# Gated recurrence and FFT gate on one core: transposes of 128 rows in place of pairs of 64 rows, with s and u in a bank each

## The chip, the cores and the metric

The kernel runs on one core of one Trainium2 chip. The metric is the device time of one execution in microseconds (us). The core's engines are named as the profile names them: PE is TensorE's matmul, PEld its load of weights, DVE VectorE, ACT ScalarE, POOL GpSimd and SP SyncE, which issues the DMAs here.

## The reference

Two layers, one after the other. The first is a gated recurrence along the sequence (6272 steps, 256 channels, 4 batches). The second multiplies two projections of its result with a circular convolution of a third one, and projects once more.

```python
def _attn_ref(x, f_logit, lower_bound):
    sig = 1.0 / (1.0 + np.exp(-f_logit))
    f = lower_bound[None, None, :] + (1.0 - lower_bound[None, None, :]) * sig
    i = 1.0 - f
    for t in range(S):
        h = f[:, t] * h + i[:, t] * x[:, t]
        y[:, t] = h

def _moe_ref(x, w_proj, filter_fft, w_out):
    proj = x @ w_proj
    x1, x2, x3 = (proj[..., :D], proj[..., D:2 * D], proj[..., 2 * D:])
    X2 = np.fft.rfft(x2, n=S, axis=1)
    H = np.fft.rfft(filter_fft, n=S, axis=0)[None, :, :]
    x2_conv = np.fft.irfft(X2 * H, n=S, axis=1)
    y = x1 * x2_conv * x3
    return y @ w_out
```

## The kernel before

All work is written as a list of operations: `op(...)` records a function, the engines that may run it and what it reads and writes. A table, `ORDER`, names for every operation its place in the program, its engine and its first PSUM bank. `emit` walks the table and calls the functions in that order, so the order on each engine and the banks are fixed by hand; `ROWS` and `ANY` name kinds of operations for a choice in `emit` that no kind uses here, since `ANY` is empty. PSUM is one tile, `PS`, of 128 x 8 banks x 512 fp32 columns. An operation with `take=1` holds one bank, one with `take=2` two neighbouring banks, `pb` and `pb + 1`. The framework adds the semaphores for what the instructions read and write.

The recurrence is `hgrn(b)`, in 13 chunks of 512 steps (the last has 128). A chunk of f_logit and one of x are loaded with 128 partitions of four consecutive steps (`FL`, `XT`, three buffers each, L321). ACT makes s = sigmoid(-f_logit) in place (L324), POOL makes u = x * s in place (L326). For each half `kh` of the channels:

- su, on PE (L338): s and u are turned, so that channels are on partitions and steps along the row. Each 128 x 128 block is turned in two transposes of 64 rows (the loop over `p`), with a 64 x 64 part of the identity. The weights that PE loads are the data; the identity streams. The output goes to every `nb`-th column (four for a full chunk). The first half of s goes to the start of the first bank and the second half to columns 256 to 511 of the second; u lies between them, across the border of the two banks: `(0, 768)` and `(512 - hn, 512)` are the columns where the halves begin, and `hn` is 256. So the two halves of a block go to different banks.
- f, on ACT (L351) or DVE (L353): f = 1 - (1 - lower_bound) * s is read from the two runs of s (`halves`) and written to `fTs`.
- scan, on DVE (L359): the recurrence itself, with f from `fTs` and u from PSUM, written as fp16 to `HA`. It begins with the last column of the chunk before. The factor (1 - lower_bound) of i is put into the weights of the second layer.
- wrap (POOL, ACT or SP): a copy of the first part of `HA` behind its end.

The second layer of batch b runs beside this: P (L707) and F1 (L720), the first steps of the transform; mini (L736) and F2 (L779), on 64 rows each; the product with the filter's spectrum (L800 on DVE, L809 on POOL); I2 (L819) and I1 (L853, on 64 rows), the inverse; x13 (L387), the two projections that are multiplied in; the product y (L859 on DVE); proj (L871) and its copy and store. The filter's own spectrum is prepared once at the start (L624, L649, L667, L684), and L595 are matmuls that keep PE at work. `hgrn(b + 1)` stands behind batch b in the list of operations, and the table mixes its operations with those of batch b: in time, transposes run from 30 to 76 us, and in the stretches 120 to 181, 220 to 281 and 300 to 380 us.

The functions that the change touches:

Of the kernel before, what the change touches and what calls it, by code (L numbers as in the profile page):

```python
# [13 lines left out]
AOP = mybir.AluOpType  # L14
AF = mybir.ActivationFunctionType
# [43 lines left out]

class Plan:  # L60

    ROWS = ("su", "F2", "mini", "I1", "FF2", "last")
    ANY = ()
    ENGINES = ("ACT", "DVE", "PE", "POOL", "SP", "MUL")

# [9 lines left out]
    def op(self, kind, cost, fn, r=(), w=(), dma=0.0, lag=0.0, table=None, take=0, src=None, part=None, margin=0.0):  # L75
        preds = set()
        for t in r:
            if t in self.writer:
                preds.add(self.writer[t])
        for t in w:  # L80
            if t in self.writer:
                preds.add(self.writer[t])
            preds.update(self.readers.get(t, ()))
        me = len(self.ops)
        if src is not None:
            preds.add(src)
            self.ops[src]["users"].append(me)
        self.ops.append(dict(kind=kind, batch=self.batch, cost=cost, fn=fn, preds=preds, dma=dma, lag=lag,
                             table=table, take=take, src=src, part=part, margin=margin, users=[]))
        for t in r:  # L90
            self.readers.setdefault(t, set()).add(me)
        for t in w:
            self.writer[t] = me
            self.readers[t] = set()
        return me
# [10 lines left out]
    def emit(self):  # L106
        rows, seen = False, set()
        for i, e, b in self.order():
# [8 lines left out]
            elif e == "PE":  # L117
                rows = o["kind"] in self.ROWS
            o["fn"](*args)
# [74 lines left out]
def kernel(  # L194
# [10 lines left out]
    nc = tc.nc  # L205
# [4 lines left out]
    op = plan.op  # L210

    konst = ctx.enter_context(tc.tile_pool(name="konst", bufs=1))
    iden = konst.tile([128, 128], F32, name="iden")
    omc = konst.tile([128, 2], F32, name="omc")
    nomc = konst.tile([128, 2], F32, name="nomc")
# [32 lines left out]
    FF2 = [("FF2", u) for u in range(NU)] + ["FF2"]  # L248
# [5 lines left out]
    PS = psp.tile([128, 8, 512], F32, name="PS")  # L254
# [23 lines left out]
    def copy(e, dst, src, scale=None):  # L278
        if e == "ACT":
            if scale is None:  # L280
                nc.scalar.copy(dst, src)  # L281
            else:
                nc.scalar.activation(dst, src, AF.Copy, scale=scale)  # L283
        elif e == "DVE":
            if scale is None:
                nc.vector.tensor_copy(dst, src)
            else:
                nc.vector.tensor_scalar(dst, in0=src, scalar1=scale, scalar2=None,
                                        op0=AOP.mult)
        elif e == "SP":  # L290
            nc.sync.dma_start(dst, src)
        else:
            nc.gpsimd.tensor_copy(dst, src)
# [5 lines left out]
    def bank(pb):  # L299

        return PS[:, pb:pb + 2].rearrange("p a t -> p (a t)")

    def halves(pb, hn):

        a = PS[:, pb, 0:hn]
        return bass.AP(tensor=a.tensor, offset=a.offset,
                       ap=[a.ap[0], [768, 2], a.ap[1]])

    count = dict(x=0, f=0, s=0, o=0, u=0, h=0)


    def hgrn(b):
        for c in range(NCHK):
            t0 = c * CH
            nb = min(CH, S - t0) // 128
            n = nb * 128
            k = count["x"] % NX
            count["x"] += 1
            xt, ft = XT[:, k, 0:nb], FL[:, k, 0:nb]
            for dst, src, t in ((ft, f_logit, ("ft", k)), (xt, x, ("xt", k))):  # L320
                op("load", {"SP": 0.46}, lambda e, dst=dst, src=src, t0=t0, n=n: nc.sync.dma_start(  # L321
                    dst, src[b, t0:t0 + n, :].rearrange("(p j) d -> p j d", p=128)),
                   w=[t], dma=0.38 * nb, lag=2.4, margin=MARGIN)
            op("sig", {"ACT": 0.095 + 0.213 * nb}, lambda e, ft=ft: nc.scalar.activation(  # L324
                ft, ft, AF.Sigmoid, scale=-1.0), w=[("ft", k)], table="sigmoid")
            op("u", {"POOL": 0.1 + 0.553 * nb}, lambda e, xt=xt, ft=ft: nc.gpsimd.tensor_tensor(  # L326
                xt, xt, ft, op=AOP.mult), r=[("ft", k)], w=[("xt", k)])
            for kh in range(2):
                cols = slice(kh * 128, kh * 128 + 128)

                hn = 64 * nb

                def turn(e, pb, ft=ft, xt=xt, cols=cols, nb=nb, hn=hn):
                    for src, at in ((ft, (0, 768)), (xt, (512 - hn, 512))):
                        for j in range(nb):
                            for p in range(2):
                                ps = slice(64 * p, 64 * p + 64)
                                nc.tensor.transpose(bank(pb)[:, at[p] + j:at[p] + hn:nb],  # L338
                                                    src[ps, j, cols], iden[ps, ps])
                su = op("su", {"PE": 0.126 * nb}, turn, r=[("ft", k), ("xt", k), "iden"], w=["qT"], take=2)  # L340
                j = count["f"] % 2
                count["f"] += 1
                fT = fTs[:, j, 0:n]
                t1 = HB[kh] + t0
                h = HA[:, t1:t1 + n]

                def gate_f(e, pb, fT=fT, hn=hn, kh=kh):
                    by, sT = nomc[:, kh:kh + 1], halves(pb, hn)
                    fT = fT.rearrange("p (a t) -> p a t", a=2)
                    if e == "ACT":  # L350
                        nc.scalar.activation(fT, sT, AF.Identity, scale=by, bias=1.0)  # L351
                    else:
                        nc.vector.tensor_scalar(fT, in0=sT, scalar1=by, scalar2=1.0,  # L353
                                                op0=AOP.mult, op1=AOP.add)
                op("f", {"ACT": 0.145 + n / 1200.0, "DVE": 0.11 + n / 960.0}, gate_f,
                   r=["om"], w=[("fT", j)], src=su)
                init = 0.0 if c == 0 else HA[:, t1 - 1:t1]
                op("scan", {"DVE": 0.12 + 2.08 * n / 1000.0}, lambda e, pb, h=h, fT=fT, hn=hn, init=init:
                   nc.vector.tensor_tensor_scan(h, fT, bank(pb)[:, 512 - hn:512 + hn], init, op0=AOP.mult,  # L359
                                                op1=AOP.add),  # L360
                   r=[("fT", j)] + ([("hn", kh, c - 1)] if c else []), w=[("hn", kh, c)],
                   src=su)

                z = min(t0 + n, WR)
                if z <= t0:
                    continue
                op("wrap", {"POOL": 0.05 + (z - t0) / 1015.0, "ACT": 0.08 + (z - t0) / 1200.0, "SP": 0.46},
                   lambda e, a=t0, z=z, o=HB[kh]: copy(
                       e, HA[:, o + S + a:o + S + z], HA[:, o + a:o + z]),
                   dma=0.5, lag=2.0,  # L370
                   r=[("hn", kh, c)], w=[("W", kh, i) for i in range(t0 // 1024, (z - 1) // 1024 + 1)])
# [514 lines left out]
    with tc.manual_schedule():  # L886
        scope = ctx.enter_context(ExitStack())
        prepare(scope.enter_context(tc.tile_pool(name="tmp", bufs=1)))
        hgrn(0)

        def turn(e):

            scope.close()
            cv = ctx.enter_context(tc.tile_pool(name="cv", bufs=1))

            late["zt"] = cv.tile([128, 2, Q, 128], F16, name="zt")
            late["Th"] = cv.tile([128, TB, 2, 64], F16, name="Th")
            late["ys"] = cv.tile([128, 2, 2, 512], F32R, name="ys")
            late["x1s"] = cv.tile([128, 2, CH], F32, name="x1s")
            late["x3s"] = cv.tile([128, 2, CH], F32, name="x3s")  # L900
            late["osb"] = [cv.tile([128, 4, 256], F32, name=f"osb{i}") for i in range(NO)]
        op("pre", {"SP": 0.01}, turn, r=FF1 + FF2 + ["ID", "VA", "FT1", "D1", "VB"], w=["cv"])

        for b in range(B):
            plan.batch = b
            spectrum(b)
            gate(b)
            phase_o(b)
            if b + 1 < B:
                plan.batch = b + 1  # L910
                hgrn(b + 1)
        plan.emit()
# [30 lines left out]
```

## Time and profile before

| what | value |
|---|---|
| median of 3 runs | 470.0 us (467.44 to 473.95) |
| the profiled execution | 470.84 us |
| its span, first to last instruction | 469.1 us |
| mean granted TensorE clock | 0.993 |
| PE, busy share of the span | 95% |
| DVE | 89% |
| ACT | 86% |
| POOL | 67% |
| PE on the transposes of s (L338, FL) | 784 matmuls, mean 230 ns |
| PE on the transposes of u (L338, XT) | 784 matmuls, mean 223 ns |
| DVE on the scan (L359) | 96 of 113.0 us, mean 1202 ns, and 8 more (the first chunks) |
| ACT on f (L351) | 90 of 59.4 us, mean 680 ns |

The span is what the trace shows of one execution; the time of the execution has 1.7 us more around it. Busy time is the union of an engine's instructions. Matmuls overlap each other, so the mean duration of one is not what it costs: this is read from the distance between the starts of two that follow each other. "A <- B: 5.2, 13, 1.1" in the list of waits means that A sat idle until B ended, 5.2 us in 13 waits, of which the longest was 1.1 us.

### The profile page before, as it was taken

To read this page: it belongs to the slowest core of one execution; us is meant where nothing else is said; L and a number is where in the kernel's file an instruction comes from. 1 tells how busy PE (TensorE), PEld (TensorE's weight loads), DVE (VectorE), ACT (ScalarE), POOL (GpSimd) and SP (SyncE) were. 2 spreads that over 40 slices of the span, in tenths; PEclk is the share of its full clock that TensorE was granted. 3 is DMA by queue.
4 is the path that set the end of the run, shared out by engine and by line. 5 is a ranking of instruction groups with operands and counts; after the bars stand their busy time and mean duration, and the time that the engine had idled before them with its cause. 6 is when DMAs were issued, how large, how long until landed. Compare 5 with 4: busy or idle time off the path is not lost.

```text
span 469.1 us, 14729 instructions
## 1 busy us (share of the span) xinstructions
PE 444.2 (95%) x6041; PEld 348.9 (74%) x6041; DVE 417.2 (89%) x477; ACT 405.4 (86%) x581; POOL 313.0 (67%) x293
## 2 busy tenths in 40 slices
PE   8779889899989999999999989999999999999998
PEld 6667666767766789777767879667778898777787
DVE  8679988599989998699999998899999987999873
ACT  4989987789989998799999987999999876999664
POOL 5988865268989854485999441878998512887700
PEclk9799999999999999999999999999999999999999
DMA  8967888957597999256787989377697831554167
GB/s 334 395 244 265 309 296 245 306 195 211 197 250 243 337 308 346 108 187 211 240 271 276 304 310 337 106 226 224 190 315 274 306 153 46 169 164 156 65 264 286
DMA packets 40417, 113.40 MB, mean 242 GB/s; under 512 B 4322, under 2 KB 6754, under 8 KB 40350
## 3 DMA queue, kind: packets, MB, share of 16 engines
q1 hardware_dynamic: 40350, 112.47, 70.1%
q8 instruction: 47, 0.77, 0.6%
q14 instruction: 20, 0.16, 0.1%
HBM read 80.93 MB, written 31.00 MB: 239 GB/s over the span
## 4 chain that ended last, share of the span: by engine, by line
PE 65%; DVE 16%; ACT 8%; issue 6%; DMA 3%; POOL 1%; ACTq 0%; DVEq 0%; POOLq 0%
PE PS L387 14%; PE PS L707 8%; PE PS L819 8%; PE PS L871 7%; DVE HA L359 7%; PE PS L338 6%; PE PS L779 6%; PE PS L720 5%; DVE ys L859 4%; DMA FL<-in_f_logit_dram 3%; PE PS L595 3%; PE PS L853 3%; PE PS L624 2%; PE PS L649 2%; ACT HA L281 2%
## 5 line engine op out<-in xcount | busy, mean ns | idle before, releaser
L326 POOL TENSOR_TENSOR XT<-XT,FL 128x1024 f32<-128x1024 f32 (+1 forms) x52 | 117.1, 2253 | 60.3 <-ACT FL L324 50.8
L359 DVE TENSOR_TENSOR_SCAN HA<-fTs,HA,PS 128x512 f16<-128x512 f32 (+1 forms) x96 | 113.0, 1202 | 4.1 <-ACT fTs L351 3.4
L800 DVE TENSOR_TENSOR PP<-PS,Hu 98x1008 f16<-98x1008 f32 x89 | 103.6, 1199 | 1.9 <-DMA Hu<-H 0.7
L387 PE MATMUL PS<-HA,W 128*128 128x490 f16 (+1 forms) x416 | 100.2, 367 | 1.7 <-ACT HA L281 0.8
L417 POOL TENSOR_TENSOR zt<-x1s,x3s 128x490 f16<-128x490 f32 (+1 forms) x48 | 58.5, 1224 | 40.2 <-DVE ys L859 11.6
L809 POOL TENSOR_TENSOR PP<-HA,Hu 98x1008 f16<-98x1008 f16 x39 | 81.8, 2105 | 2.7 <-ACT HA L281 1.7
L281 ACT CAST HA<-PS 128x1024 f16<-128x1024 f32 (+1 forms) x90 | 75.4, 865 | 7.8 <-PE PS L720 4.8
L859 DVE TENSOR_TENSOR ys<-PS,zt 128x1024 fp32r<-128x1024 f32 (+1 forms) x52 | 58.7, 1154 | 4.6 <-PE PS L853 2.5
L351 ACT ACTIVATE fTs<-PS,nomc 128x512 f32<-128x512 f32 (+1 forms) x90 | 59.4, 680 | 2.8 <-PE PS L338 1.6
L283 ACT ACTIVATE osb<-PS 128x1024 f32<-128x1024 f32 (+1 forms) x52 | 50.4, 981 | 13.1 <-PE PS L871 6.6
L387 PEld LDWEIGHTS <-W 128*128 128x128 f16 x416 | 35.6, 97 | 33.9 <-issue 7.3
L324 ACT ACTIVATE FL<-FL 128x1024 f32<-128x1024 f32 (+1 forms) x52 | 53.0, 1020 | 8.9 <-DMA FL<-in_f_logit_dram 8.9
L871 PE MATMUL PS<-Wo,ys 128*128 128x256 f32 x392 | 56.8, 291 | 0.2 <-DVE ys L859 0.2
L819 PEld LDWEIGHTS <-PP 98*128 98x128 f16 x1024 | 49.3, 98 | 10.1 <-issue 3.1
L283 ACT ACTIVATE x1s<-PS 128x490 f32<-128x490 f32 (+1 forms) x87 | 50.6, 591 | 5.2 <-PE PS L387 3.8
L819 PE MATMUL PS<-VA,PP 98*128 98x98 f16 x512 | 51.9, 207 | 0.6 <-DVE HA L359 0.5
L871 PEld LDWEIGHTS PS<-Wo,ys 128*128 128x128 f32 x392 | 49.1, 188 | 4.0 <-DVE ys L859 0.6
L819 PE MATMUL PS<-VB,PP 98*128 98x98 f16 x512 | 51.6, 207 | 0.0
L281 ACT CAST Th<-PS 128x784 f16<-128x784 f32 x57 | 46.9, 829 | 3.1 <-PE PS L819 2.2
L338 PE MATMUL PS<-iden,FL 64*128 64x64 f32 x784 | 44.7, 230 | 3.9 <-DVE HA L359 1.5
L338 PEld LDWEIGHTS PS<-iden,FL 64*128 64x128 f32 x784 | 33.5, 138 | 16.9 <-DVE HA L359 5.2
L707 PE MATMUL PS<-W,HA 128*128 128x256 f16 x392 | 44.3, 273 | 1.8 <-ACT X L281 1.8
(114 smaller groups left out, 744.9 us busy)
## 6 DMA issues: line engine op xcount, KB each, us to landing
FL<-in_f_logit_dram SPq DMA_DIRECT2D x48, 512.0 KB
XT<-in_x_dram SPq DMA_DIRECT2D x48, 512.0 KB
out_dram<-osb SPq DMA_DIRECT2D x48, 512.0 KB
Hu<-H SPq DMA_DIRECT2D x55, 392.0 KB
X<-in_moe_filter_fft_dram SPq DMA_DIRECT2D x9, 512.0 KB
H<-Hu SPq DMA_DIRECT2D x8, 196.0 KB
Hu<-in_moe_filter_fft_dram SPq DMA_DIRECT2D x2, 512.0 KB
H<-Hu SPq DMA_DIRECT2D x8, 128.0 KB
```

The source lines that it names most:

```text
L281: nc.scalar.copy(dst, src)
L283: nc.scalar.activation(dst, src, AF.Copy, scale=scale)
L326: op("u", {"POOL": 0.1 + 0.553 * nb}, lambda e, xt=xt, ft=ft: nc.gpsimd.tensor_tensor(xt, xt, ft, op=AOP.mult), r=[("ft", k)], w=[("xt", k)])
L338: nc.tensor.transpose(bank(pb)[:, at[p] + j:at[p] + hn:nb], src[ps, j, cols], iden[ps, ps])
L359: nc.vector.tensor_tensor_scan(h, fT, bank(pb)[:, 512 - hn:512 + hn], init, op0=AOP.mult, op1=AOP.add),
L387: nc.tensor.matmul(PS[:, p, 0:n], W13[:, kh, js], HA[:, HB[kh] + t0:HB[kh] + t0 + n], start=(kh == 0), stop=(kh == 1))
L707: nc.tensor.matmul(pp[:, r - r0, :], column(HB[kh], q_of(r)), W2[:, kh, :], start=(kh == 0), stop=(kh == 1))
L800: nc.vector.tensor_tensor(pr, px.unsqueeze(1).broadcast_to([TB, 2, UE, 63]), hh, op=AOP.mult)
L809: nc.gpsimd.tensor_tensor(pr, spec[:, o, :, 1:64].unsqueeze(1).broadcast_to([TB, 2, UE, 63]), hh, op=AOP.mult)
L819: nc.tensor.matmul(PS[:, ib + o, pr * TB:(pr + 1) * TB], PP[:TB, k, o, n, 2 * pr:2 * pr + 2, :], v[:TB], start=(n == 0), stop=(n == 1))
L859: nc.vector.tensor_tensor(late["ys"][:, yk, :, 0:rn * 128], PS[:, cb:cb + 2, 0:rn * 128], late["zt"][:].rearrange("p k r m -> p k (r m)") ...
L871: nc.tensor.matmul(po[:, i, :], late["ys"][:, yk, kh, i * 128:(i + 1) * 128], Wo[:, kh, :], start=(kh == 0), stop=(kh == 1))
```

## The change

Each block is turned by one transpose of all 128 rows with the whole identity, 128 columns of it. All of s goes to the first bank of the operation's two, all of u to the second. f reads the first bank alone and the scan the second alone, each in one run of 512 columns. `part=0` and `part=1` say so in the list of operations; `emit` doesn't use them. The order table, with its places, engines and banks, stays as it is, and so do all other operations.

```diff
-    ROWS = ("su", "F2", "mini", "I1", "FF2", "last")
+    ROWS = ("F2", "mini", "I1", "FF2", "last")
...
-                hn = 64 * nb
-
-                def turn(e, pb, ft=ft, xt=xt, cols=cols, nb=nb, hn=hn):
-                    for src, at in ((ft, (0, 768)), (xt, (512 - hn, 512))):
+                def turn(e, pb, ft=ft, xt=xt, cols=cols, nb=nb, n=n):
+                    for i, src in enumerate((ft, xt)):
                         for j in range(nb):
-                            for p in range(2):
-                                ps = slice(64 * p, 64 * p + 64)
-                                nc.tensor.transpose(bank(pb)[:, at[p] + j:at[p] + hn:nb],
-                                                    src[ps, j, cols], iden[ps, ps])
+                            nc.tensor.transpose(PS[:, pb + i, j:n:nb], src[:, j, cols], iden[:])
...
-                def gate_f(e, pb, fT=fT, hn=hn, kh=kh):
-                    by, sT = nomc[:, kh:kh + 1], halves(pb, hn)
-                    fT = fT.rearrange("p (a t) -> p a t", a=2)
+                def gate_f(e, pb, fT=fT, n=n, kh=kh):
+                    by = nomc[:, kh:kh + 1]
                     if e == "ACT":
-                        nc.scalar.activation(fT, sT, AF.Identity, scale=by, bias=1.0)
+                        nc.scalar.activation(fT, PS[:, pb, 0:n], AF.Identity, scale=by, bias=1.0)
                     else:
-                        nc.vector.tensor_scalar(fT, in0=sT, scalar1=by, scalar2=1.0,
+                        nc.vector.tensor_scalar(fT, in0=PS[:, pb, 0:n], scalar1=by, scalar2=1.0,
                                                 op0=AOP.mult, op1=AOP.add)
                 op("f", {"ACT": 0.145 + n / 1200.0, "DVE": 0.11 + n / 960.0}, gate_f,
-                   r=["om"], w=[("fT", j)], src=su)
+                   r=["om"], w=[("fT", j)], src=su, part=0)
                 init = 0.0 if c == 0 else HA[:, t1 - 1:t1]
-                op("scan", {"DVE": 0.12 + 2.08 * n / 1000.0}, lambda e, pb, h=h, fT=fT, hn=hn, init=init:
-                   nc.vector.tensor_tensor_scan(h, fT, bank(pb)[:, 512 - hn:512 + hn], init, op0=AOP.mult,
+                op("scan", {"DVE": 0.12 + 2.08 * n / 1000.0}, lambda e, pb, h=h, fT=fT, n=n, init=init:
+                   nc.vector.tensor_tensor_scan(h, fT, PS[:, pb + 1, 0:n], init, op0=AOP.mult,
                                                 op1=AOP.add),
                    r=[("fT", j)] + ([("hn", kh, c - 1)] if c else []), w=[("hn", kh, c)],
-                   src=su)
+                   src=su, part=1)
```

More of the change, by code (lines that the diff above doesn't have):

```diff
@@ L301, in bank @@
         return PS[:, pb:pb + 2].rearrange("p a t -> p (a t)")
[L303 to L307, printed above, removed]
     count = dict(x=0, f=0, s=0, o=0, u=0, h=0)
```

## The prediction

> **What bounds the kernel now.** I read the page first, part 1 and the chain in part 4, then the busy time by stage, then the rows of the transposes beside those of other matmuls, then the timeline, then the list of waits.
>
> ```profile
> PE 444.2 (95%) x6041; PEld 348.9 (74%) x6041; DVE 417.2 (89%) x477; ACT 405.4 (86%) x581; POOL 313.0 (67%) x293
> ...
> PE 65%; DVE 16%; ACT 8%; issue 6%; DMA 3%; POOL 1%; ACTq 0%; DVEq 0%; POOLq 0%
> ```
>
> PE is busiest, and 65% of the chain that ended last is PE. The ends of matmuls are modelled, so I counted PE's own work from starts: matmuls of a line by their steady spacing (207 ns on L387 with 490 columns, 109 on L707 with 256, 56 on L720 with 128, 43.5 on L819 with 98, 118 on L871, 62.4 per pair on L338). That is 392 us. Changes between matmuls on 64 rows (L338, L779, L736, L853, L667, L684) and on more rows, 226 of them, add 21 us (below). About 52 us are waits, 24 of them before 91 us. So from 91 us on PE has some 28 us of slack in 378: what PE does longer, the kernel mostly takes longer.
>
> ```profile
> 120.00:181.00 61.00, 57.74 (x934) 44.78 (x932) 58.82 (x62) 56.30 (x84) 46.98 (x36) 1.00 0.85 276
> 220.00:281.00 61.00, 58.90 (x934) 45.97 (x933) 58.38 (x59) 58.12 (x91) 45.79 (x35) 1.00 0.81 273
> 300.00:380.00 80.00, 79.33 (x1237) 60.59 (x1236) 78.57 (x83) 76.20 (x116) 64.12 (x54) 1.00 0.77 256
> ```
>
> Columns are window, length, then PE, PEld, DVE, ACT, POOL busy (count), granted clock, DMA share, GB/s. Three of the four stretches that hold transposes are here (the fourth is 30 to 76 us, in the preparation). DVE too is 96 to 98% busy in them: the stages have two bounds, and part of a PE delay falls where PE would have waited for DVE anyway.
>
> **What a transpose costs.** Today a 128x128 block is turned as two halves of 64 rows, which run at the same time on the two row halves of PE; each streams a 64-column identity. Afterwards it is one transpose that streams 128 columns. There are 784 pairs now (1568 matmuls on L338), 784 transposes after.
>
> ```profile
> 156.31 0.41 PE L338 MATMUL PS<-iden,FL 64*128 64x64 f32 x8
> 156.56 0.41 PE L338 MATMUL PS<-iden,XT 64*128 64x64 f32 x8
> 156.81 0.41 PE L338 MATMUL PS<-iden,FL 64*128 64x64 f32 x8
> 157.06 0.41 PE L338 MATMUL PS<-iden,XT 64*128 64x64 f32 x8
> ```
>
> Eight transposes, four pairs, start every 0.25 us: 62.4 ns a pair. What fills them: the streaming or the load of the weights?
>
> ```profile
> L338 PEld LDWEIGHTS PS<-iden,FL x784: 134/138/143, 30.1 to 379.4; 64*128 64x128 f32 x196
> L338 PE MATMUL PS<-iden,FL x784: 214/223/275, 30.1 to 379.4; 64*128 64x64 f32 x196
> ...
> L853 PE MATMUL PS<-ID,Th x784: 212/216/228, 155.4 to 461.7; 64*128 64x128 f16 x196
> ...
> L720 PE MATMUL PS<-D,X x512: 216/219/230, 93.6 to 430.8; 128*128 128x128 f16 x171
> ...
> L819 PE MATMUL PS<-VA,PP x512: 203/207/218, 100.9 to 441.2; 98*128 98x98 f16 x171
> ```
>
> Between L819 (98 columns, 207 ns) and L387 (490 columns, 370 ns) a column is worth 0.416 ns. By that 64 columns should show 193 ns. They show 223, as much as 128 to 136 columns of fp16. Modelled ends could mislead, but the semaphore events agree: an operation's end is signalled 220 ns after its last start on L819, 231 on L853 (128 columns), 287 on L707 (256), and 242 on L338. And the first matmul of the other kind follows 145 ns after the last start on L853, 155 after that on L338. So a 64-column fp32 transpose, with its output spread at a step of four, takes some 53 ns: about 0.83 ns a column. The load takes about 54: after a change of kind the second load starts 51 to 60 ns after the first. Load and stream are in balance now; with 128 columns the stream is 107 ns and the load, 128 columns either way, stays at 54 behind it.
>
> With what spacing adds above streaming (2 to 11 ns: 109 on L707, 118 on L871, 62.4 against 53) I take **112 ns** a transpose. Ends: 56 (L720, a full-array matmul of 128 columns) and 125 (twice the pair). Term 1: 784 x (112 - 62.4) = **+38.9 us** of PE work, between -5 and +49.
>
> The Trainium skill, "TensorE: Matmul & The Clock Gate", section Terms, says that transposes have a mode that makes fp32 four times as fast; with the four passes that "FP8 and Floating Point Precision" gives plain fp32, that is one pass, so 128 columns would cost what they cost in fp16, 53 ns by rows. The 223 ns and 242 ns above speak against it; by it term 1 would be 0, since the load then binds. It is rival B.
>
> **Changes between row kinds.** L387 to L387 starts follow in 206 ns, L387 to L338 in 300; L720 to itself 56, to L338 150; L338 to itself 62, to L387 155. A change costs 94 ns, and the first fp32 load behind it another 48. Counted along PE's order, with L338 moved to the full-row side, 226 changes become 204: -22 x 0.094 = **-2.1 us**. The exposed loads stay: 33 entries pay now (from L387, L871, L819 and others), 34 would (from L853, L779, L667, L736).
>
> **Banks.** f and scan now both read both banks, and of an operation's transposes only the last signals, so anything that needs either bank waits for the scan. Afterwards the first bank is free when f ends, over 1 us earlier. What PE waits for that scan:
>
> ```profile
> PEld PS L338 <- DVE HA L359: 5.2, 13, 1.1
> ...
> PE PS L338 <- DVE HA L359: 1.5, 3, 0.6
> PE PS L853 <- DVE HA L359: 1.1, 4, 0.5
> ```
>
> With the small ones 9.1 us. The next transposes of s could go ahead in the free bank while the scan ends, so at most the 6.7 us of L338 is gone; single-bank users could save some of the rest. With a slower PE these waits shrink anyway. I take **-2 us**, between 0 and -9. The order table is the same, so nothing runs earlier than its place on PE allows.
>
> **Start of f.** It waits for all 16 halves now, 0.50 us; it would wait for four transposes, 4 x 112 = 0.45 us. The u half, another 0.45, is covered by f itself (0.70 us). So the link to the scan grows by nothing: **0** (a gain of 0.25 us an operation in rival B).
>
> **Readers.** f takes 698 ns for 512 columns in two runs, the scaled copy on L283 598 for 490, or 625 at 512; in one run f may lose 73 ns: up to 85 x 0.073 = 6 us of ACT. ACT is 8% of the chain: -0.5 at most; I take 0. The scan (1268 ns) reads the same count in one run as before.
>
> **Loads.** The three buffers of s and u come free when the second transposes end, up to 0.9 us later a chunk. ACT's waits for f_logit (8.9 us, 8 times) can grow by that, 8 x 0.9 = 7 us off PE; the other chunks have the buffers as cover. I take 0, up to +3.
>
> **What is absorbed.** 196 transposes, 9.7 us, fall into each of the four stretches. In the first PE's idle time is large (24 us): I take 6 of 9.7 as absorbed. In the other three PE waits 19 us beside 202 us; I let 8 of 29 vanish there, under half of the waits, since PE runs in a fixed order and a wait is seldom where the delay is. Sum: 38.9 - 2.1 - 2 - 14 = **+21 us**. The profiled execution took 470.84 us (span 469.1 and 1.7 around it), 0.2% above the median of 470.0. So 470.84 + 21 = **492 us**. Its own range is 480 (22 more absorbed, or less stream) to 506.
>
> **Rivals.**
> B, not slower: a full transpose costs no more than a pair. The place is L338; the mechanism, the weight load as the bound, decides if 128 columns stream in under 62 ns. For it: load and pair are in step (a load starts 6 ns after a pair does), and the load does not grow; if the two halves share one path, 223 ns would be their common time and one full stream would fit. Against it: row-half pairs on L853 share nothing (128 columns in 56 ns). Time: 470.8 - 2.1 - 3.5 = **465**, and 460 with all bank waits gone.
> C, hidden: the change does what I say on PE, but DVE (58.8 of 61 us) is the true bound and only 2 us a stretch show: 470.8 + 8 - 2 = **477**.
> D, worse: in full-row form the load isn't hidden behind the stream, 54 + 107 = 161 ns: 784 x 0.099 = +77, less 14 and 4: **530**. Against it: L871, a full-row fp32 load of 188 ns, has a spacing of 118 beside 256 columns.
>
> **How the numbers follow.** Mine 0.66, B 0.24, C 0.05, D 0.05. The predicted time is mine, 492. The range reaches to B and holds most of it: 463 to 508; left out are D, the fast end of B and the top of mine. About 2% is what a measurement here can tell from no change. Faster by more (below 460.6): the end of B, 0.07. Within: the rest of B, C and a little of mine, 0.23. Slower: 0.70.
>
> **What would show it.** L338 with 784 matmuls, 128x128, records near 280 ns, and starts 105 to 118 ns apart: term 1. At 56 to 64 ns B is right; near 160, D. Each operation signals twice, and f starts half an operation after its first transpose. Waits of L338 for L359 fall below 3 us. PE's waits in the three stretches fall by a third or more, and each stretch is 4 to 8 us longer; if PE's spacing is 112 and the stretches grow by under 3 us each, C. A DVE more idle than now shows PE as the bound.

## The result and the profile after

The changed kernel takes 484.61 us (median of 4 runs, 483.81 to 485.4) beside 470.94 for the kernel before, measured beside it: a ratio of 1.0293, 95% interval 1.0216 to 1.0369. It is slower by 13.7 us, where 21 were forecast. The profiled execution took 485.05 us, its span is 483.3, which is 14.2 us more than the 469.1 before.

Lines of the file shift by 10 to 12: the transposes are on L328 now, f on L339 (ACT) and L341 (DVE), the scan on L347. From the page of the changed kernel, busy time and the chain by engine:

```profile
PE 468.2 (97%) x5257; PEld 377.1 (78%) x5257; DVE 420.5 (87%) x477; ACT 409.5 (85%) x581; POOL 313.5 (65%) x293
...
PE 84%; ACT 7%; DVE 4%; DMA 2%; issue 2%; POOL 0%; SPq 0%; DVEq 0%; ACTq 0%; POOLq 0%
```

The chain went from 65% PE to 84% PE, and DVE's part from 16% to 4%: by the chain there is one bound now, which e13_scan_after tests below. The three stretches of the changed kernel, with the columns as in the prediction:

```profile
120.00:181.00 61.00, 60.02 (x694) 49.87 (x692) 57.26 (x57) 54.42 (x82) 47.72 (x36) 1.00 0.75 257
220.00:281.00 61.00, 60.94 (x708) 48.63 (x705) 55.49 (x57) 56.25 (x86) 44.10 (x34) 1.00 0.78 264
300.00:380.00 80.00, 79.11 (x956) 61.54 (x955) 73.17 (x80) 73.16 (x108) 66.16 (x56) 1.00 0.67 218
```

PE is busy for 60.0 and 60.9 of 61 us and 79.1 of 80; DVE fell from 96 to 98% to 91 to 94%, ACT from 92 to 95% to 89 to 92%. The granted clock is 1.00 in these stretches in both kernels. The rows of the transposes and their timeline:

```profile
L328 PEld LDWEIGHTS PS<-iden,FL x392: 137/140/145, 30.1 to 392.9; 128*128 128x128 f32 x196
L328 PE MATMUL PS<-iden,FL x392: 270/273/332, 30.1 to 393.0; 128*128 128x128 f32 x196
```

```profile
153.69 0.60 PE L328 MATMUL PS<-iden,XT 128*128 128x128 f32 x4
154.13 0.60 PE L328 MATMUL PS<-iden,FL 128*128 128x128 f32 x4
154.57 0.60 PE L328 MATMUL PS<-iden,XT 128*128 128x128 f32 x4
```

Four transposes take 0.44 us, 109 ns each, with a record of 273 ns: just the values of L707 before, an fp16 matmul of 256 columns.

```profile
L707 PE MATMUL PS<-W,HA x392: 269/273/329, 79.1 to 392.7; 128*128 128x256 f16 x196
```

The load of the weights, 140 ns in its record beside 138, didn't grow. Three waits of the changed kernel:

```profile
ACT fTs L339 <- PE PS L328: 5.0, 16, 0.7
DVE HA L347 <- ACT fTs L339: 4.9, 15, 0.6
...
PEld PS L328 <- DVE HA L347: 1.2, 3, 0.4
```

The kernel before has these for f and the scan:

```profile
ACT fTs L351 <- PE PS L338: 1.6, 7, 0.3
DVE HA L359 <- ACT fTs L351: 3.4, 6, 1.0
```

The loads of the transposes wait 1.2 us for scans in place of 5.2, and their matmuls no longer do (1.5 us before). f waits more for PE than before, and the scan more for f.

Counted from starts as in the prediction, PE's account is:

| us | before | after |
|---|---|---|
| PE's own work | 392.2 | 428.8 |
| changes of row kind (number) | 21.2 (226) | 19.2 (204) |
| the rest, taken as waits | 52.0 | 31.6 |
| sum | 465.4 | 479.6 |

So 36.6 us of work came, 2.0 of changes went, and of the waits 20.4 us went: together 14.2, the difference of the spans. Where it shows, measured from the first matmul of P (L707, after L695) of one batch to that of the next: +2.1 us up to the first, then +1.2, +4.4, +6.0, and +0.6 to the end.

### The profile page after: what moved, and what is told of

The parts are those of the page before. It is cut to its first block, busy times and chain, and to the rows that moved or that the text cites. A ratio compares the mean times of both kernels' runs of the same rounds, so it can differ in the third digit from the quotient of the medians.

```text
span 483.3 us, 13243 instructions
## 1 busy us (share of the span) xinstructions
PE 468.2 (97%) x5257; PEld 377.1 (78%) x5257; DVE 420.5 (87%) x477; ACT 409.5 (85%) x581; POOL 313.5 (65%) x293
## 4 chain that ended last, share of the span: by engine, by line
PE 84%; ACT 7%; DVE 4%; DMA 2%; issue 2%; POOL 0%; SPq 0%; DVEq 0%; ACTq 0%; POOLq 0%
PE PS L328 17%; PE PS L375 16%; PE PS L859 9%; PE PS L807 9%; PE PS L695 8%; PE PS L767 6%; PE PS L708 5%; PE PS L841 5%; PE PS L637 3%; PE PS L583 3%; ACT f L281 2%; PE PS L655 1%; DMA FL<-in_f_logit_dram 1%; DVE X L286 1%; ACT HA L281 1%
## 5 line engine op out<-in xcount | busy, mean ns | idle before, releaser
L347 DVE TENSOR_TENSOR_SCAN HA<-fTs,HA,PS 128x512 f16<-128x512 f32 (+1 forms) x96 | 113.1, 1203 | 6.8 <-ACT fTs L339 4.9
L375 PE MATMUL PS<-HA,W 128*128 128x490 f16 (+1 forms) x416 | 99.2, 367 | 0.6 <-ACT X L283 0.6
L339 ACT ACTIVATE fTs<-PS,nomc 128x512 f32<-128x512 f32 (+1 forms) x90 | 59.8, 676 | 6.0 <-PE PS L328 5.0
L328 PE MATMUL PS<-iden,FL 128*128 128x128 f32 x392 | 62.3, 279 | 1.3 <-ACT afs L281 0.4
L328 PE MATMUL PS<-iden,XT 128*128 128x128 f32 x392 | 59.7, 273 | 0.0
L328 PEld LDWEIGHTS PS<-iden,FL 128*128 128x128 f32 x392 | 43.9, 140 | 12.0 <-issue 1.6
```

What stands on the lines that cost most here:

```text
L328: nc.tensor.transpose(PS[:, pb + i, j:n:nb], src[:, j, cols], iden[:])
L339: nc.scalar.activation(fT, PS[:, pb, 0:n], AF.Identity, scale=by, bias=1.0)
L347: nc.vector.tensor_tensor_scan(h, fT, PS[:, pb + 1, 0:n], init, op0=AOP.mult, op1=AOP.add),
L375: nc.tensor.matmul(PS[:, p, 0:n], W13[:, kh, js], HA[:, HB[kh] + t0:HB[kh] + t0 + n], start=(kh == 0), stop=(kh == 1))
```

## The experiments

Two theories stood after the result. Theory 1: the 20 us of waits went because PE had more to do, and the separate banks are worth little. Theory 2: the separate banks took most of them away. Each run has the kernel before beside it on its chip; ratios are to that.

**e7_half: the banks at PE's old cost.** In the changed kernel:

```diff
-    nc.tensor.transpose(PS[:, pb + i, j:n:nb], src[:, j, cols], iden[:])
+    nc.tensor.transpose(PS[:, pb + i, j:64 * nb:nb], src[0:64, j, cols], iden[0:64, 0:64])
```

with f reading `PS[:, pb, 0:n // 2]` twice and the scan `PS[:, pb + 1, 0:1]` n times.

> The changed kernel, with only the first 64 rows of each block turned (one transpose of 64 rows that streams 64 columns, in place of one of 128 that streams 128); f reads its 256 columns twice and the scan one column 512 times, so every reader has as much to read as before, and half of the steps are left out. PE's work on transposes should be that of the kernel before (784 starts about 62 ns apart), the banks of s and u stay apart. So this run shows what the separate banks are worth at the old cost of PE. Theory 1 (the waits that went away were mostly covered by PE's longer work, the banks are worth only the waits on the scan): 463 to 469 us, 2 to 8 below the kernel before. Theory 2 (the separate release itself took 14 us or more off): 453 to 458 us. If the spacing stays at 109 ns, the cost of a transpose does not come from the columns streamed.

Measured: 470.57 us, ratio 1.0023 (0.9985 to 1.0060). Starts are 62 to 63 ns apart: the cost fell with the columns streamed, and one half alone costs what a pair of halves does in the kernel before (62.4). The list of waits of this kernel (the transposes are on L336, the scan on L355) has two entries of transposes for the scan:

```profile
PEld PS L336 <- DVE HA L355: 0.5, 2, 0.4
...
PE PS L336 <- DVE HA L355: 0.2, 1, 0.2
```

The kernel before has 5.2 and 1.5. So most of these waits are gone, and nothing is won in the time. Both theories missed. Part of it may be the clock: in the profiled execution 10 us at half the granted clock lie just ahead of the first phase P (last section), and it begins at 83.5 us where the kernel before has 79.1. If the clock is all of these 4.4 us, the span of 471.9 would be 1.6 below the 469.1 of before without them. The two runs of e7_half with a granted clock of 0.993, as in the profiled execution of the kernel before, took 469.95 and 469.68 us, beside a median of 469.6: no gain there either. So at the old cost of PE the separate banks bring some 2 us or less.

**e6_twice: PE's new work without the banks.** In the kernel before:

```diff
-    for p in range(2):
+    for p in (0, 1, 0, 1)[:4 if j < nb - 1 else 2]:
```

> The kernel before (pairs of 64 rows, both banks held by f and scan), with three of the four pairs of each full chunk issued twice: 576 pairs more at 62.4 ns, 35.9 us more work on PE, as much as the change added (36.6), but without its banks. Theory 1: PE's waits cover 12 to 16 us of it as in the changed kernel, 490 to 496 us. Theory 2 (the separate release saved 14 us or more in the changed kernel): 498 to 506 us. At 486 or less the banks did nothing at all.

Measured: 491.11 us, ratio 1.0474 (1.0416 to 1.0532). Of 35.9 us of work, 21.5 show and 14.4 are covered; beside the added work only f's start is later. That is theory 1's range. It is also 6.5 us above the changed kernel (6.2 above e4_apart, next, which ran on the same chip), which has 0.7 us more PE work; 2.0 of that are the fewer changes of row kind. What the rest is, the next runs ask.

**e3_joint and e4_apart: the release alone, at PE's new cost.** In the changed kernel, behind the scan (e3; e4 has `pb + 1`):

```diff
+    nc.vector.tensor_copy(seen[:, 0:1], PS[:, pb, 0:1])
```

> The changed kernel with a copy of one column on DVE behind each scan, which reads the first bank (that of s), so that this bank too is free only after the scan, as before the change. To be compared with the next run, whose copy reads the second bank and leaves the release as changed; the copies themselves, 104 of some 0.1 us, stand on DVE in both. Theory 1: 2 to 6 us above the next run, 488 to 494 us. Theory 2: 10 us or more above it.

> The changed kernel with a copy of one column on DVE behind each scan, which reads the second bank (that of u), so the banks are released apart as in the changed kernel. Both theories: 485 to 489 us; PE is the bound, and 104 copies of about 0.1 us on DVE hardly show.

Measured: 486.72 us, ratio 1.0390 (1.0336 to 1.0444), and 484.93, ratio 1.0349 (1.0302 to 1.0397). Both lie just below their ranges. The difference of 1.8 us is small, and the intervals overlap: the release of the first bank is worth 2 us or nothing, not 10.

**e9_u_first: the early start of f.** In the changed kernel:

```diff
-    for i, src in enumerate((ft, xt)):
+    for i, src in ((1, xt), (0, ft)):
```

> The changed kernel with u turned ahead of s, so that f, which needs all of s, can start only after all eight transposes (0.87 us from the operation's start) in place of four (0.44 us). Nothing else differs; in the run with pairs issued twice f also starts 0.87 us late. Theory 1 (the early start of f is what makes the changed kernel cheaper than that run, beyond 2 us for fewer changes of row kind and 2 us for the banks): 2 to 5 us above the changed kernel, 487 to 490 us. Theory 2 (f is covered anyway): within 1 us of the changed kernel, 484 to 485.5 us.

Measured: 489.17 us, ratio 1.0407 (1.0370 to 1.0444), 4.6 us above the changed kernel, in theory 1's range. The comparison with it is across two sets of runs; e1 below, with the changed kernel's order and work, has 1.0307 (1.0275 to 1.0339), and these intervals don't meet. The waits of f and the scan in this kernel, and those of the transposes' loads for u:

```profile
ACT fTs L339 <- PE PS L328: 19.2, 41, 1.2
DVE HA L347 <- ACT fTs L339: 10.7, 25, 0.8
...
PEld PS L328 <- POOL XT L320: 3.1, 7, 0.6
```

and in e6_twice, where f starts as late:

```profile
ACT fTs L351 <- PE PS L338: 18.2, 45, 1.2
DVE HA L359 <- ACT fTs L351: 10.5, 27, 0.7
```

Against 5.0 and 4.9 us for f and the scan in the changed kernel. So f and the scan do wait for the late s. But something else differs too: u, which POOL makes from s, is turned first here, and PE's loads wait 3.1 us for it; the changed kernel has no such wait in its list. So the 4.6 us are not wholly the early start of f. The distance between e6_twice and the changed kernel gives another figure: 6.5 + 0.7 - 2.0 for the changes of row kind, less up to 1.8 for the release, leaves 3.4 to 5.2, a remainder and not a measurement. What the separate banks bring at PE's new cost is then mostly that s, complete in its own bank, is signalled after four transposes: some 3 to 5 us.

**e1_contig and e2_fp16: what the 109 ns are.** In the changed kernel, e1:

```diff
-    nc.tensor.transpose(PS[:, pb + i, j:n:nb], src[:, j, cols], iden[:])
+    nc.tensor.transpose(PS[:, pb + i, j * 128:j * 128 + 128], src[:, j, cols], iden[:])
```

and e2, with s and u as the fp16 halves of FL's words (`part16`):

```diff
-    nc.tensor.transpose(PS[:, pb + i, j:n:nb], src[:, j, cols], iden[:])
+    nc.tensor.transpose(bank16(pb + i)[:, j * 128:j * 128 + 128],
+                        part16(ft, 1 - i)[:, j, cols], iden16[:])
```

> The changed kernel with each transpose writing 128 neighbouring columns of its bank in place of every fourth; f and the scan read the same columns as before, so the steps come in another order than the reference's. Theory 1 (the 109 ns of a transpose are its 128 fp32 columns, at 0.83 ns each, and the load is hidden): starts stay 109 ns apart and the time stays at 484 to 486 us. Theory 2 (the output's step of four costs it): starts 56 to 62 ns apart and 463 to 471 us.

> The changed kernel with s and u written as fp16 into the two halves of the words of FL (by ACT and POOL as before), turned as fp16 with an fp16 identity into neighbouring columns; f and scan read fp16. The steps come in another order than the reference's. Theory 1 (fp32 costs two streaming steps a column): starts 56 ns apart, 784 x 53 = 41.5 us less PE work than the changed kernel, and since the kernel before with only 7 us more PE work takes 470, DVE is then nearly the bound: 462 to 469 us. If the transpose as such is slow, whatever the type, starts stay at 109 ns and the time at 485.

Measured: e1 484.57 us, ratio 1.0307 (1.0275 to 1.0339), starts 109 ns apart; e2 471.8 us, ratio 1.0026 (0.9994 to 1.0058), starts 56 ns apart. Their rows of transposes, e1 and e2:

```profile
L328 PE MATMUL PS<-iden,FL x392: 270/273/332, 30.3 to 393.8; 128*128 128x128 f32 x196
```

```profile
L337 PE MATMUL PS<-iden,FL x784: 216/219/232, 30.2 to 381.2; 128*128 128x128 f16 x196
```

The step of four in the output costs nothing. fp32 does: 128 columns take 109 ns in fp32 and 56 in fp16. The time of e2 missed its range of 462 to 469: PE has 5 us less work on transposes than the kernel before and 22 fewer changes, and the time is that of the kernel before.

**e8_packed: half of the transposes.** In the kernel before, s and u become the upper and lower fp16 of one word:

```diff
-    for src, at in ((ft, (0, 768)), (xt, (512 - hn, 512))):
-        for j in range(nb):
-            for p in range(2):
-                ps = slice(64 * p, 64 * p + 64)
-                nc.tensor.transpose(bank(pb)[:, at[p] + j:at[p] + hn:nb],
-                                    src[ps, j, cols], iden[ps, ps])
+    for j in range(nb):
+        for p in range(2):
+            ps, at = slice(64 * p, 64 * p + 64), (512 - hn, 512)[p]
+            nc.tensor.transpose(bank(pb)[:, at + j:at + hn:nb], ft[ps, j, cols], iden[ps, ps])
```

> The kernel before with s and u written as fp16 into the upper and the lower half of the same fp32 word (by ACT and POOL), so that one fp32 transpose turns both: 392 pairs of 64 rows in place of 784, in the columns that u had, across the border of the two banks; f reads every second fp16 from the upper halves, the scan from the lower ones. If a transpose passes the 32 bits on as they are, the outputs are the reference's within fp16's rounding of s and u. 392 x 62.4 = 24.5 us less PE work than the kernel before. Theory 1 (two bounds, DVE at 96 to 98% in the three stretches): the gain is 6 to 14 us, 456 to 464 us. If PE alone were the bound: 446 to 450.

Measured: 471.27 us, ratio 1.0017 (0.9993 to 1.0041). A miss: 24.5 us less work on PE, and no gain. In its first stretch

```profile
120.00:181.00 61.00, 53.10 (x741) 39.27 (x740) 59.26 (x62) 58.07 (x85) 47.69 (x36) 1.00 0.85 276
```

PE fell from 57.7 to 53.1 us and DVE stayed at 59 of 61. The edit also adds a wait: a transpose now needs u as well as s, and its loads wait for POOL, where the kernel before has one such wait of 0.5 us:

```profile
PEld PS L345 <- POOL FL L334: 9.6, 17, 1.7
```

How much of the missing gain that is wasn't separated. No run beats the kernel before by 2%.

**e10_dose: a third of e6's work.** As e6_twice, for one `j` of four.

> The kernel before with one of the four pairs of each full chunk issued twice: 192 pairs more, 12.0 us of PE work, a third of the earlier dose (35.9 us, which cost 21.5 us). Theory 1 (the kernel before stands at a knee: PE's waits take up the first microseconds whole): 471 to 474 us. Theory 2 (each microsecond on PE costs 0.6, at any dose): 476 to 478 us.

Measured: 474.37 us, ratio 1.0105 (1.0068 to 1.0143), 4.6 us for 12.0. It lies between the two ranges, close to theory 1's. From 12.0 to 35.9 us of work the distance to the kernel before rises by 16.9 us. So a microsecond more on PE costs 0.39 at first and 0.71 later, and one less (e8) brought nothing.

**e11_light, e12_scan_packed, e13_scan_after: what holds 470.** e11 and e12 start from e8, e13 from the changed kernel. e11 computes f on a quarter of its columns; e12 and e13 do half of each scan:

```diff
-    nc.vector.tensor_tensor_scan(h, fT, words(pb, hn, 0), init, ...)
+    nc.vector.tensor_tensor_scan(h[:, 0:hn], fT[:, 0:hn], words(pb, hn, 0)[:, 0:hn], init, ...)
+    nc.vector.memset(h[:, hn:2 * hn], 0.0)
```

> The kernel with s and u in one word (24.5 us less PE work than before, 471 us), with f computed on a quarter of its columns (128 of 512) and the scan reading one column of f 512 times: about 0.33 us less per f, 30 us less ACT work, most of f left out. It asks what held that kernel at 471 us when PE had become lighter. If ACT is the floor there: 455 to 464 us. If DVE or the fixed order is: 469 to 472 us.

> The kernel with s and u in one word (24.5 us less PE work than before, 471 us), with each scan over the first half of its columns and the other half of the result set to zero by a DVE memset: about 0.45 us less a chunk and half, 40 to 50 us less DVE work; half of the recurrence is left out. If DVE is what holds that kernel at 471 us: 445 to 460 us. If the fixed order or the chain of single waits holds it: 467 to 471 us.

> The changed kernel with the same half scans (half of the recurrence left out), 40 to 50 us less DVE work. If PE is the only bound of the changed kernel, as its chain says (84% PE): 480 to 484 us, 1 to 4 below it. If DVE bounds it too: below 475 us.

Measured: e11 467.65 us, ratio 0.9949 (0.9926 to 0.9972); e12 469.71, ratio 1.0009 (0.9978 to 1.0039); e13 484.46, ratio 1.0312 (1.0266 to 1.0358). The first stretch of e11, and the three of e12:

```profile
120.00:181.00 61.00, 54.23 (x749) 40.98 (x747) 59.35 (x63) 54.01 (x85) 46.40 (x36) 1.00 0.86 286
```

```profile
120.00:181.00 61.00, 50.67 (x724) 38.06 (x722) 49.48 (x86) 56.97 (x83) 46.13 (x36) 1.00 0.87 272
220.00:281.00 61.00, 55.13 (x734) 40.21 (x735) 49.22 (x81) 59.02 (x89) 45.89 (x35) 1.00 0.80 271
300.00:380.00 80.00, 75.01 (x1023) 54.19 (x1022) 69.69 (x105) 76.88 (x116) 64.84 (x57) 1.00 0.78 252
```

and the first of e13:

```profile
120.00:181.00 61.00, 60.03 (x698) 49.65 (x693) 49.25 (x82) 54.43 (x82) 48.01 (x37) 1.00 0.75 255
```

e13, just above its range for PE alone (480 to 484), shows that DVE doesn't bound the changed kernel: with DVE at 49 of 61 us the time doesn't move. With PE at 60 of 61 us, and 84% of the chain, that leaves PE; ACT, at 89 to 92% there, was not lightened. The floor at 470 is no single engine's: PE with 24.5 us less (e8), that and DVE with 7 to 10 us less in each stretch (e12, in the range for the fixed order), or that and ACT with 29 us less on f (e11, a miss between its two ranges) leave it within 1%. In e12 ACT is the busiest, at 93 to 97%; in e11 DVE is, at 96 to 97%. Both also keep e8's waits for POOL. Whether it is ACT and DVE together, these waits or the fixed order of all engines was not tried.

Pairs of 64 rows with s and u in a bank each weren't tried.

## Why the prediction was right, and what was mis-sized

The range, 463 to 508 us, held rivals B and C too, so a time inside it would not have told them apart; the 109 ns and PE's account do.

**A transpose, +38.9 us.** 784 transposes at 109 ns in place of 112: 36.6. The reading of the 223 ns record and the 242 ns signal as two fp16 columns for each fp32 one is shown by e1 and e2. Rival B falls, with 109 ns and not 56 to 64. So does D: the load is hidden, 109 and not 161 ns. The trace shows the load by itself where nothing holds it back: the second load of an operation starts some 60 ns after the first, the later ones every 109. Whether load or stream sets the 62 ns of 64 columns wasn't separated. On "TensorE: Matmul & The Clock Gate", section Terms, of the Trainium skill, which as the prediction reads it would have had 128 columns at their fp16 cost: the trace doesn't agree; fp32 is 109 ns beside 56, twice and not the same. Whether the mode that the page names was on, no run here shows.

**Changes of row kind, -2.1 us.** 204, as counted: -2.0.

**Banks, -2 us.** The release alone is 1.8 us at the new cost of PE (not clear of noise), and at the old one all that the separate banks bring is some 2 us or less. The waits that e7 takes from the list were not gain. The step's bound of 6.7 us counted 1.5 twice, too: the three waits of matmuls for the scan stand at the same moments (33.4, 51.6 and 137.8 us) as waits of their loads.

**Start of f, 0.** s is complete after 0.44 us beside 0.50, as the step said; f and the scan still wait 3.4 and 1.5 us more than before, and what that costs wasn't separated. What the step didn't say is that this start, more than the release, is what the separate banks are for: some 3 to 5 us (e9 and e6).

**Readers and loads, 0.** f's median is 689 ns in both kernels, so reading in one run won nothing. ACT's waits for f_logit fell from 8.9 to 4.1 us, where up to 7 more were feared.

**What is absorbed, -14 us.** This is the term that was mis-sized. The waits fell by 20.4 us; with 1.8 for the release some 18.6 are absorbed, where the step had 14. e6 covers 14.4 in a kernel that also starts f late; with 3 to 5 for that start the two agree. The error lies in the first two stretches: the step let 6 of 9.7 us vanish in the first, where 7.6 did, and a third at most in the next, where the growth was 1.2 us. In the last two, 4.4 and 6.0 us, it was nearer to its 7. So of the three stretches, which were to be 4 to 8 us longer, the first stayed within the 3 us that were rival C's sign. C's mechanism isn't shown by that: DVE is 94% busy there after the change, PE 98%, and e13 takes DVE's load away without a gain. What the row of the kernel before does show is slack, PE at 57.7 of 61 us in that stretch beside 79.3 of 80 in the last.

The sum by measured terms: 36.6 - 2.0 - 20.4 = 14.2 us, where the forecast had 38.9 - 2.1 - 16. The errors point the same way, so no luck of one against another is in the result.

## What to carry to other kernels

A transpose on PE cost here by the columns of identity that it streams and their type: 128 columns took 109 ns in fp32 and 56 in fp16. Two fp32 half transposes side by side on the two halves of the rows stream half as many each and took 62.4 ns together, so the split that looks like twice the instructions is the cheaper one. This kernel, whose order was fixed around several engines at 95%, stands at a knee: work added to PE cost 0.4 to 0.7 of itself, and work taken from PE, alone or with DVE or ACT, brought under 1%. Taking work from all three at once was not tried. Where two results share a buffer, look at which is signalled first: the reader's early start was worth more here, some 3 to 5 us, than the buffer's early release, 2 us or nothing.

## What the runs showed of the hardware beyond that

In e7_half PE has the same number of starts as after the change, but half the array's rows in use, and its profiled execution ran at half the granted clock in three stretches, 16.8 to 23.6, 33.8 to 37.2 and 71.4 to 81.6 us. The profiled execution of the kernel before had one such stretch in the preparation, 16.2 to 23.0. The clock row of e7_half's page, in 40 slices:

```profile
PEclk9799995999999999999999999999999999999999
```

and of the kernel before:

```profile
PEclk9799999999999999999999999999999999999999
```

The stretches of e7_half last 3.4, 6.8 and 10.2 us, one, two and three times the same length. A light PE doesn't explain them by itself: e8_packed has three such stretches too, the last from 54.2 to 61.0 us, but e12_scan_packed, with as few transposes, has none after 23.7 us, and e10_dose, with more than the kernel before, has one at 72.1 us. What sets the clock back in the preparation wasn't tried.
